# Denominators of a linear-attention pair: summed over partitions by a turn through memory instead of by TensorE

## The chip, the cores and the metric

One core of one Trainium2 chip runs the whole program. The metric is the device time of one execution in microseconds (us); the time given for a kernel is the median of several executions. Engines: TensorE (PE in the profile, PEld its weight loads), VectorE (DVE), ScalarE (ACT), GpSimd (POOL) and SyncE (SP). SP, ScalarE and GpSimd each have a queue from which they start transfers (DMA); all transfers share 16 DMA engines.

## The reference

Two independent attention blocks A and B, with S = 2048 rows, D = 640 and 32 heads of 20, whose outputs stand side by side:

```python
qkv = (x @ wqkv).reshape(B, S, 3, H, Dh).transpose(2, 0, 3, 1, 4)
phi = lambda t: where(t > 0, t + 1, exp(t)) + 1e-6
pq, pk = phi(q), phi(k)
kv  = einsum("bhsd,bhse->bhde", pk, v);  z = einsum("bhsd->bhd", pk)
num = einsum("bhqd,bhde->bhqe", pq, kv)
den = einsum("bhqd,bhd->bhq", pq, z)[..., None] + 1e-6
out = (num / den).transpose(0, 2, 1, 3).reshape(B, S, D) @ wo
```

The denominator `den` is one number for each row and head: a sum over 20 products of phi(q) and z.

## The kernel before

Every large product is made of three TensorE products of numbers cut into a high and a low part (tiles ending in h and l). The first 285 us build keys, values and z for both blocks, and the matrix M = kv times wo. The part that matters here comes after: eight units u = 0 to 7 (`NU` = 8), each of 512 rows, four of block A and four of block B.

For each unit there are two stretches on TensorE.

- The q stretch (`qmm`, L912 to L914): five column blocks c, each with five steps k of three products into one bank `psq`. ScalarE and VectorE make phi of each block (`qphi`), and `qacc` adds phi times z over the blocks into `acc[u]`, 128 partitions x 512 rows. The weights are ordered so that a partition p holds head p modulo 32: the denominator of head h is the sum of partitions h, h+32, h+64 and h+96 of `acc`.
- The o stretch (`outmm`, L1191): the division result times M, in 14 steps s = 0 to 13 of 6 products (s 0 to 5) or 9 products (s 6 to 13). The products of half q of the rows accumulate in the bank pa[q]. After steps 0 and 1, 4 and 5, 8 and 9, 10 and 11 ScalarE copies that bank out (L1206, `o<-pa`), and the accumulation goes on in it: step 10 writes the bank that the copy after step 8 reads, and step 11 the one of the copy after step 9.

The program runs q(u), then o(u-1): so after q(1) comes o(0), after q(2) comes o(1). The denominator of unit v is made during o(v-1), the stretch behind its own q stretch, and is used in o(v), one stretch pair later. The order is written by hand: `at(("o", w, s), f, ...)` puts a step f behind step s of o(w), and `run` calls it there. Each engine works off its own instructions strictly in that order.

The steps for one unit before:

- `split_acc`: ScalarE rounds `acc` (L906 `ac<-acc`), VectorE takes the remainder (L903).
- `denmm`: two TensorE products with `same`, a 128 x 128 matrix that is 1 where two partitions have the same head (L1102, L1103). The bank `psd` then holds the denominator in all four partitions of the head, for all 512 rows.
- `recip`: two VectorE reciprocals of 256 columns (L1108) into `rd`.
- `divide`: two VectorE products of 5 x 256 columns (L1114) on phi(q).
- Then `d_sums`, `a_split`, `d_split` prepare the left factors of o(v).

`round_xq` (L950 `xqh<-xqs`) rounds the next unit's input on ScalarE after steps 4, 6, 8, 10 and 12; q of the next unit needs the five results one after the other from its start on. SP loads these inputs (`xqs`, L943) and their low parts (`xql`, L947).

Each transfer of SP and of ScalarE raises one of eight semaphores, DMAHW0 to DMAHW7, which are handed out in turn over both queues. A transfer that takes a semaphore first waits until the earlier transfer with the same one has landed.

Of the kernel before, what the change touches and what calls it, by code (L numbers as in the profile page):

```python
# [7 lines left out]
F32 = mybir.dt.float32  # L8
# [3 lines left out]
AF = mybir.ActivationFunctionType  # L12
OP = mybir.AluOpType

H = 32
# [60 lines left out]
class Plan:  # L76
# [9 lines left out]
    def note(self, engine, n, fn, w, r, ahead=None, dma=None, late=None, by=None, due=None, safe=0.0):  # L86
        base = self.RATE.get(engine)
        j = Job(engine, base[0] + base[1] * n if base else n, fn, ahead, dma)
        for part, writes in [(p, True) for p in w] + [(p, False) for p in r]:
            sp = part.space  # L90
            if sp.where is not None and sp not in j.spaces:
                j.spaces.append(sp)
            for lo, hi, other, wrote in sp.uses:
                if lo < part.hi and part.lo < hi and (writes or wrote) and other is not j:
                    j.deps.add(other)
            if writes:
                sp.uses = [u for u in sp.uses if not (part.lo <= u[0] and u[1] <= part.hi and u[2] is not j)]
# [12 lines left out]
        self.jobs.append(j)  # L110
        return j
# [104 lines left out]
def tile_linear_attn_pair(ctx: ExitStack, tc: tile.TileContext, ins, out: bass.AP):  # L216
    nc = tc.nc
    P = 128
# [7 lines left out]
    NU = NB * NG  # L226
# [7 lines left out]
    dram = ctx.enter_context(tc.tile_pool(name="dram", bufs=1, space=bass.MemoryType.DRAM))  # L234
# [3 lines left out]
    kx, kg, q1a, q1b, q2, q3 = [], [], [], [], [], []  # L238
# [430 lines left out]
    a, z, x = jh[0][0:P], jl[0][0:P], jr[0][0:P]  # L669
# [117 lines left out]
    for p in range(4, NPB):  # L787
        i, h = divmod(p - 2, 2)
# [9 lines left out]
    for p in range(NPB + 2, NP):  # L798
        i, h = divmod(p - NPB - 2, 2)
# [17 lines left out]
    j = note("HOST", 0.0, swap, [gate.all], [])  # L817
# [51 lines left out]
    for g, (h0, nh) in enumerate(GROUPS):  # L869
        cols = NC * DH * nh  # L870
        w = Space("wv", cols, (BD,))
# [17 lines left out]
    def bank(name, tag="one", bufs=3):  # L889
        at, n = ptags[tag]  # L890
        pn[tag] = pn.get(tag, -1) + 1
        return psum.tile([P, 512], F32, name=name, tag=f"bank{at + pn[tag] % n}", bufs=1)
# [163 lines left out]
            nc.sync.dma_start(f32(t)[:, cs], d)  # L1056

    pq, acc, den, dd = {}, {}, {}, {}

    def qmm(u, c):  # L1060
        b = u // NG
        ps = bank("psq")
        cs = slice(c * P, (c + 1) * P)
        for k in range(NC):
            wh, wl = whl["q", b, k]
            xh, xl = xt[u, k]
            mm3(ps, wh[:, cs], wl[:, cs], xh, xl, k == 0, k == NC - 1)
            run("q", u, c, k)
        if c == NC - 1:
            for k in range(NC):  # L1070
                xt.pop((u, k))
        return ps
# [26 lines left out]
    def denmm(u):  # L1099
        t = acc.pop(u)  # L1100
        ps = den.pop(u) if u in den else bank("psd", "small", 1)
        nc.tensor.matmul(ps, same, t[:, 0], start=True, stop=False)  # L1102
        nc.tensor.matmul(ps, same, t[:, 1], start=False, stop=True)  # L1103
        den[u] = (ps, q2[0].tile([P, 512], F32, name="rd", tag="rd", bufs=1))

    def recip(u, h):
        ps, r = den[u]
        nc.vector.reciprocal(r[:, h * 256:(h + 1) * 256], ps[:, h * 256:(h + 1) * 256])  # L1108
# [169 lines left out]
    h = NG - 1  # L1278
# [8 lines left out]
    for c in range(NC):  # L1287
# [3 lines left out]
        for u in range(1, NU - 1):  # L1291
# [5 lines left out]

    chain = {
        0: [(("q", 1, 0, 0), split_acc, 0), (("q", 1, 1, 1), denmm, 0), (("q", 1, 1, 1), recip, 0, 0),
            (("q", 1, 1, 1), recip, 0, 1), (("q", 1, 1, 2), divide, 0, 0), (("q", 1, 1, 4), divide, 0, 1),  # L1300
            (("q", 1, 2, 0), d_sums, 0, 0), (("q", 1, 2, 2), a_split, 0, 0), (("q", 1, 2, 4), d_sums, 0, 1),
            (("q", 1, 3, 1), d_split, 0, 0), (("q", 1, 3, 4), a_split, 0, 1), (("q", 1, 4, 1), d_split, 0, 1)]}
    for v in range(1, NU):
        w, u = v - 1, v + 1
        if v == NU - 1:
            chain[v] = [(("o", w, 1), split_acc, v), (("o", w, 4), denmm, v), (("o", w, 4), recip, v, 0),
                        (("o", w, 5), divide, v, 0), (("o", w, 6), a_split, v, 0, 0), (("o", w, 6), d_sums, v, 0, 0),
                        (("o", w, 7), d_split, v, 0, 0), (("o", w, 8), a_split, v, 1, 0), (("o", w, 8), d_sums, v, 1, 0),
                        (("o", w, 9), recip, v, 1), (("o", w, 10), d_split, v, 1, 0), (("o", w, 12), divide, v, 1),
                        (("o", v, 0), a_split, v, 0, 1), (("o", w, 13), d_sums, v, 0, 1),  # L1310
                        (("o", v, 0), d_split, v, 0, 1), (("o", v, 2), d_sums, v, 1, 1),
                        (("o", v, 2), a_split, v, 1, 1), (("o", v, 3), d_split, v, 1, 1)]
        elif v == 1:
            chain[v] = [(("o", w, 4), split_acc, v), (("o", w, 7), denmm, v), (("o", w, 8), recip, v, 0),
                        (("o", w, 10), recip, v, 1), (("o", w, 11), divide, v, 0),
                         (("o", w, 12), divide, v, 1), (("q", u, 0, 2), d_sums, v, 0), (("q", u, 0, 4), a_split, v, 0),
                         (("q", u, 1, 2), d_sums, v, 1), (("q", u, 2, 1), d_split, v, 0), (("q", u, 3, 1), a_split, v, 1),
                         (("q", u, 3, 4), d_split, v, 1)]
        else:
            chain[v] = [(("o", w, 2), split_acc, v), (("o", w, 5), denmm, v), (("o", w, 7), recip, v, 0),  # L1320
                        (("o", w, 9), recip, v, 1), (("o", w, 11), divide, v, 0),
                         (("o", w, 12), divide, v, 1), (("q", u, 0, 2), d_sums, v, 0), (("q", u, 0, 4), a_split, v, 0),
                         (("q", u, 1, 2), d_sums, v, 1), (("q", u, 2, 1), d_split, v, 0), (("q", u, 3, 1), a_split, v, 1),
                         (("q", u, 3, 4), d_split, v, 1)]
    for v in range(NU):
        for a, f, *x in chain[v]:
            at(a, f, *x)
# [63 lines left out]
```

## Time and profile before

| | |
|---|---|
| time, median of 3 runs (571.76 to 574.32) | 573.65 us |
| the profiled execution's own time | 574.53 us |
| its span, first to last instruction | 572.8 us |
| TensorE busy | 565.7 us, 99% |
| VectorE busy | 434.3 us, 76% |
| ScalarE busy | 341.4 us, 60% |
| GpSimd busy | 57.2 us, 10% |
| granted TensorE clock | 0.999 |

The 1.73 us between the profiled execution's time and its span lie before the first and behind the last instruction. A unit's q and o stretches together take 33.34 us in the middle of the second part.

### The profile page before, as it was taken

Reading aid. Unit: us, or ns where it says so; the run is one execution under the profiler, and the core shown is the slowest. Engines: PE = TensorE matmul, PEld = TensorE weight load, DVE = VectorE, ACT = ScalarE, POOL = GpSimd, SP = SyncE. Lnnn points to the kernel's source line nnn. Section 1 sums busy time; section 2 is a strip of 40 time slices with the busy share of each in tenths; the row PEclk is TensorE's granted clock in tenths of the full one; section 3 lists DMA queues with packets and bytes.
Section 4 is the critical chain, followed back from the end, with each engine's and each line's share of the span. In section 5 each row is a group of like instructions: output and inputs, shape, how many; then the busy total and the mean of one; then the engine's idle time right before and its main releaser. Section 6 shows DMA issues by size and latency. Waiting matters only on the chain.

```text
span 572.8 us, 9505 instructions
## 1 busy us (share of the span) xinstructions
PE 565.7 (99%) x3524; PEld 535.8 (94%) x3524; DVE 434.3 (76%) x706; ACT 341.4 (60%) x619; POOL 57.2 (10%) x93
## 2 busy tenths in 40 slices
PE   8999999999999999999999999999999999999997
PEld 6999999999999999999988899898989989898997
DVE  6788687599888589976555699967788786758792
ACT  6877566673786677655156665646556464644551
POOL 0210011110010011100000103120012201001010
PEclk9999999999999999999999999999999999999999
DMA  8994665758858889786787986663363996122022
GB/s 296 379 242 141 163 183 128 205 143 246 278 144 217 250 249 321 216 252 196 211 245 275 339 276 215 226 218 109 120 225 134 355 390 231 47 76 93 0 93 92
DMA packets 69441, 117.64 MB, mean 205 GB/s; under 512 B 7956, under 2 KB 31252, under 8 KB 69396
## 3 DMA queue, kind: packets, MB, share of 16 engines
q1 hardware_dynamic: 60500, 89.98, 48.2%
q0 software_dynamic: 8608, 26.88, 16.7%
q8 instruction: 27, 0.44, 0.3%
q10 hardware_dynamic: 288, 0.20, 0.1%
q14 instruction: 18, 0.15, 0.1%
HBM read 71.13 MB, written 35.41 MB: 186 GB/s over the span
## 4 chain that ended last, share of the span: by engine, by line
PE 89%; DMA 5%; DVE 3%; ACT 1%; issue 1%; SPq 1%; ACTq 0%; DVEq 0%
PE psg L312 20%; PE pa L1191 12%; PE ka L312 8%; PE psq L912 8%; PE psq L914 8%; PE psq L913 8%; PE pe L1191 6%; PE ke L312 4%; PE psk L711 4%; PE psb L1191 4%; PE kb L312 3%; DMA md<-mev 2%; DMA wk<-in_A_wk 1%; PE pskv L551 1%; PE pskv L972 1%; DMA xqs<-in_A_xt 1%
## 5 line engine op out<-in xcount | busy, mean ns | idle before, releaser
L312 PE MATMUL psg<-pkl,xnh 128*128 128x320 f32 x320 | 98.9, 309 | 0.0
L312 PE MATMUL psg<-pkh,xnh 128*128 128x320 f32 x320 | 98.8, 309 | 0.0
L312 PE MATMUL psg<-pkh,xnl 128*128 128x320 f32 x320 | 98.4, 308 | 0.0
L912 PE MATMUL psq<-xqh,wh 128*128 128x512 f32 x200 | 78.6, 393 | 1.0 <-ACT xqh L860 1.0
L914 PE MATMUL psq<-xqh,wl 128*128 128x512 f32 x200 | 78.0, 390 | 0.0
L913 PE MATMUL psq<-xql,wh 128*128 128x512 f32 x200 | 77.9, 390 | 0.0
L312 PEld LDWEIGHTS psg<-pkl,xnh 128*128 128x128 f32 x320 | 60.1, 188 | 0.0
L312 PEld LDWEIGHTS psg<-pkh,xnl 128*128 128x128 f32 x320 | 60.1, 188 | 0.0
L312 PEld LDWEIGHTS psg<-pkh,xnh 128*128 128x128 f32 x320 | 60.0, 188 | 0.0
L1206 ACT ACTIVATE o<-pa 128x320 f32<-128x320 f32 x64 | 27.9, 438 | 45.2 <-PE pa L1191 45.0
L484 ACT ACTIVATE kt<-ka 128x320 f32<-128x320 f32 x52 | 22.6, 435 | 52.2 <-PE ka L312 49.0
L1082 DVE SCALAR_TENSOR_TENSOR pq<-eq,rq 128x512 f32<-128x512 f32 x40 | 27.6, 691 | 30.7 <-ACT rq L1081 30.6
L401 POOL DMA_DIRECT2D zacc<-ek x32 | 26.4, 836 | 244.5 <-DVE ek L494 185.3
L532 DVE TENSOR_TENSOR gacc<-psg,gacc 128x320 f32<-128x320 f32 x60 | 29.4, 489 | 28.1 <-PE psg L312 27.3
L1080 ACT ACTIVATE eq<-psq 128x512 f32<-128x512 f32 x40 | 23.9, 597 | 36.6 <-PE psq L914 34.2
L912 PEld LDWEIGHTS psq<-xqh,wh 128*128 128x128 f32 x200 | 37.6, 188 | 8.5 <-ACT xqh L860 1.3
L914 PEld LDWEIGHTS psq<-xqh,wl 128*128 128x128 f32 x200 | 37.5, 188 | 7.9
L913 PEld LDWEIGHTS psq<-xql,wh 128*128 128x128 f32 x200 | 37.6, 188 | 7.2
L396 ACT ACTIVATE pkh<-ek,epst 128x640 fp32r<-128x640 f32 x32 | 26.5, 829 | 7.9 <-DVE ek L494 7.5
L1191 PE MATMUL pa<-fh,dah 128*128 128x320 f32 x96 | 29.7, 309 | 0.0
L1191 PE MATMUL pa<-fh,dal 128*128 128x320 f32 x96 | 29.7, 309 | 0.0
L1191 PE MATMUL pa<-fl,dah 128*128 128x320 f32 x96 | 29.7, 309 | 0.0
(213 smaller groups left out, 1553.3 us busy)
## 6 DMA issues: line engine op xcount, KB each, us to landing
zacc<-ek POOLq DMA_DIRECT2D x32, 320.0 KB, 5.8
xql<-xd SPq DMA_DIRECT2D x40, 256.0 KB, 5.9
xd<-xl SPq DMA_DIRECT2D x29, 320.0 KB, 6.2
out<-o POOLq DMA_DIRECT2D x28, 320.0 KB, 3.6
xns<-in_A_x SPq DMA_DIRECT2D x16, 320.0 KB, 5.8
xts<-in_B_xt_tiles SPq DMA_DIRECT2D x16, 320.0 KB, 4.3
xns<-in_B_x SPq DMA_DIRECT2D x16, 320.0 KB, 5.1
xqs<-in_A_xt SPq DMA_DIRECT2D x20, 256.0 KB, 6.0
```

Of the source, the lines that this page charges most:

```text
L312: nc.tensor.matmul(o, a.r, w.r, start=start and k == i == 0, stop=k == n - 1 and i == 2, skip_group_check=True)
L396: note("ACT", n + 110, lambda: act(hi.r, p.f, AF.Identity, bias=epst), [hi], [p, K0.all], by=8.0)
L401: note("POOL", 1.0, lambda: nc.gpsimd.dma_start(z.f, p.f, **kw), [z], [p], dma=1.0 if first else 1.86)
L532: tt(o, BK[k].tile[:, :HF], o, op=OP.add)
L711: nc.tensor.matmul(o[h][:, :HF], x[a].r, w[c][h * HF:h * HF + HF].r, start=c == 0 and i == 0, stop=c == NC - 1 and i == 2, skip_group_chec ...
L912: nc.tensor.matmul(o, whi, xhi, start=first, stop=False)
L913: nc.tensor.matmul(o, whi, xlo, start=False, stop=False)
L914: nc.tensor.matmul(o, wlo, xhi, start=False, stop=last)
L1080: nc.scalar.activation(e, ps, AF.Exp)
L1082: nc.vector.scalar_tensor_tensor(pq[u][:, c, :], e, 1.0, r, op0=OP.min, op1=OP.add)
L1191: nc.tensor.matmul(ps, x, y, start=start and n == i == 0, stop=n == len(terms) - 1 and i == 2, skip_group_check=True)
L1206: copy = lambda x, y: nc.scalar.activation(x, y, AF.Copy)
```

## The change

For units 1 to 6 the sum over the four partitions is made in another way. Units 0 and 7 keep `split_acc`, `denmm` and `recip`.

- `acc_out`: one transfer from ScalarE's queue writes `acc` (128 x 512, 256 KB) to a tensor `ad` in memory.
- `acc_turn`: four transfers from ScalarE's queue read it back, each into 32 partitions, 64 KB in runs of 512 bytes. Partition q*32+h then holds, for head h and for the 128 rows of quarter q, the four numbers that belong together, side by side.
- `acc_add`: VectorE adds 256 columns to 256 columns, then 128 to 128, and takes the reciprocal of 128 columns.
- `spread`: each quarter's 32 x 128 reciprocals are copied to the four groups of 32 partitions of `rd`. VectorE makes the eight copies of quarters 2 and 3, ScalarE the eight of quarters 0 and 1.
- `divide` stays, one step later for the second half.

```diff
+    def acc_out(u):
+        nc.scalar.dma_start(ad[u], acc[u])
+        den[u] = (None, q2[0].tile([P, 512], F32, name="rd", tag="rd", bufs=1))
+
+    def acc_turn(u):
+        v = ad[u].rearrange("(k h) (q j) -> q h k j", k=4, q=4)
+        for q in range(4):
+            nc.scalar.dma_start(acc[u][q * H:q * H + H].rearrange("p (k j) -> p k j", k=4), v[q])
+
+    def acc_add(u):
+        t = acc[u]
+        nc.vector.tensor_tensor(t[:, :256], t[:, :256], t[:, 256:], op=OP.add)
+        nc.vector.tensor_tensor(t[:, :P], t[:, :P], t[:, P:256], op=OP.add)
+        nc.vector.reciprocal(t[:, :P], t[:, :P])
+
+    def spread(u, g, copy):
+        t = acc[u][g * H:g * H + H, :P]
+        for k in range(4):
+            copy(den[u][1][k * H:k * H + H, g * P:g * P + P], t)
...
-        elif v == 1:
-            chain[v] = [(("o", w, 4), split_acc, v), (("o", w, 7), denmm, v), (("o", w, 8), recip, v, 0),
-                        (("o", w, 10), recip, v, 1), (("o", w, 11), divide, v, 0),
-                         (("o", w, 12), divide, v, 1), (("q", u, 0, 2), d_sums, v, 0), (("q", u, 0, 4), a_split, v, 0),
...
-            chain[v] = [(("o", w, 2), split_acc, v), (("o", w, 5), denmm, v), (("o", w, 7), recip, v, 0),
-                        (("o", w, 9), recip, v, 1), (("o", w, 11), divide, v, 0),
...
+            o = 1 if v == 1 else 0
+            chain[v] = [(("o", w, 3 + o), acc_out, v), (("o", w, 6 + o), acc_turn, v), (("o", w, 10), acc_add, v),
+                        (("o", w, 10), spread_v, v, 2), (("o", w, 11), spread_v, v, 3),
+                        (("o", w, 11), spread_a, v, 0), (("o", w, 11), spread_a, v, 1),
+                        (("o", w, 12), divide, v, 0), (("o", w, 13), divide, v, 1),
```

What stands on the engines is shown at three places. In the rows, `psb` and `pa` are banks of the o stretch, and a name in brackets is a semaphore that the instruction waits for (DMAHW: transfers of SP and ScalarE; DMASW: of GpSimd).

TensorE in o(0), between steps 7 and 8, before:

```order
L1191 MATMUL psb<-fh,dah 128x320
L1191 MATMUL psb<-fl,dah 128x320
L1191 MATMUL psb<-fh,dal 128x320
L1102 MATMUL psd<-ac,same 128x512
L1103 MATMUL psd<-ac,same 128x512
L1191 MATMUL pa<-fh,dsh 128x320
L1191 MATMUL pa<-fl,dsh 128x320
```

and now (the line of `outmm` has become L1222):

```order
L1222 MATMUL psb<-fh,dah 128x320
L1222 MATMUL psb<-fl,dah 128x320
L1222 MATMUL psb<-fh,dal 128x320
L1222 MATMUL pa<-fh,dsh 128x320
L1222 MATMUL pa<-fl,dsh 128x320
```

The two products with `same` are gone, and nothing takes their place; the same holds in o(1) to o(5).

ScalarE in o(0), from the copy after step 4 to the rounding after step 8, before:

```order
L1206 ACTIVATE o<-pa 128x320 [waits PE_49]
L950 ACTIVATE xqh<-xqs 128x512 [waits DMAHW7_49]
L906 ACTIVATE ac<-acc 128x512 [waits DVE_49]
L1206 ACTIVATE o<-pa 128x320 [waits PE_49]
L950 ACTIVATE xqh<-xqs 128x512 [waits DMAHW0_49]
L906 ACTIVATE fsh<-wst 128x640 [waits DMAHW1_49,DVE_49]
L1206 ACTIVATE o<-pa 128x320 [waits DMASW4_49,PE_49]
L950 ACTIVATE xqh<-xqs 128x512
```

and now:

```order
L1237 ACTIVATE o<-pa 128x320 [waits PE_49]
L950 ACTIVATE xqh<-xqs 128x512 [waits DMAHW7_49]
L1108 DMA ad_3790<-acc 128x512 [waits DMAHW7_49,DVE_49]
L1237 ACTIVATE o<-pa 128x320 [waits PE_49]
L950 ACTIVATE xqh<-xqs 128x512 [waits DMAHW0_49]
L906 ACTIVATE fsh<-wst 128x640 [waits DMAHW1_49,DVE_49]
L1115 DMA acc<-ad_3790 32x4x128 [waits DMAHW7_49,DMAHW0_49]
L1115 DMA acc<-ad_3790 32x4x128
L1115 DMA acc<-ad_3790 32x4x128 [waits DMAHW2_49]
L1115 DMA acc<-ad_3790 32x4x128 [waits DMAHW3_49]
L1237 ACTIVATE o<-pa 128x320 [waits DMASW4_49,PE_49]
L950 ACTIVATE xqh<-xqs 128x512
```

The store stands where the rounding of `acc` stood; the four turned loads stand ahead of the copy after step 8, and the first of them waits until the store has landed (DMAHW7).

ScalarE in o(3), from the rounding of a form of M to the copy after step 8, now:

```order
L906 ACTIVATE fsh<-wst 128x640 [waits DMAHW1_49,DMASW6_49]
L1108 DMA ad_3793<-acc 128x512 [waits DMAHW6_49,DVE_49]
L1237 ACTIVATE o<-pa 128x320 [waits PE_49]
L950 ACTIVATE xqh<-xqs 128x512 [waits DMAHW2_49]
L1237 ACTIVATE o<-pa 128x320 [waits PE_49]
L950 ACTIVATE xqh<-xqs 128x512 [waits DMAHW3_49]
L1115 DMA acc<-ad_3793 32x4x128 [waits DMAHW6_49]
L1115 DMA acc<-ad_3793 32x4x128 [waits DMAHW4_49]
L1115 DMA acc<-ad_3793 32x4x128
L1115 DMA acc<-ad_3793 32x4x128 [waits DMAHW0_49]
L1237 ACTIVATE o<-pa 128x320 [waits DMASW4_49,PE_49]
```

where before stood:

```order
L906 ACTIVATE ac<-acc 128x512 [waits DVE_49]
L906 ACTIVATE fsh<-wst 128x640 [waits DMAHW2_49,DMASW6_49]
L1206 ACTIVATE o<-pa 128x320 [waits PE_49]
L950 ACTIVATE xqh<-xqs 128x512 [waits DMAHW3_49]
L1206 ACTIVATE o<-pa 128x320 [waits PE_49]
L950 ACTIVATE xqh<-xqs 128x512 [waits DMAHW4_49]
L1206 ACTIVATE o<-pa 128x320 [waits DMASW4_49,PE_49]
```

The fourth turned load of unit 4 takes DMAHW0, which the first of the five `xql` loads for unit 5 had before it: ScalarE cannot go on before that load of SP has landed. The rounding of the form (`fsh`) has moved ahead of the step that waits for `acc`.

More of the change, by code (lines that the diff above doesn't have):

```diff
@@ L1058, in tile_linear_attn_pair @@
     pq, acc, den, dd = {}, {}, {}, {}
+    ad = {u: dram.tile([P, 512], F32, name=f"ad{u}") for u in range(1, NU - 1)}
     def qmm(u, c):
@@ L1104, in denmm, with spread_a, spread_v @@
         den[u] = (ps, q2[0].tile([P, 512], F32, name="rd", tag="rd", bufs=1))
+    def acc_out(u):
[14 more added lines that the diff above has]
+            copy(den[u][1][k * H:k * H + H, g * P:g * P + P], t)
+        if g == 1:
+            acc.pop(u)
+    def spread_a(u, g):
+        spread(u, g, lambda y, x: nc.scalar.activation(y, x, AF.Copy))
+    def spread_v(u, g):
+        spread(u, g, nc.vector.tensor_copy)
     def recip(u, h):
@@ L1312, in tile_linear_attn_pair @@
                         (("o", v, 2), a_split, v, 1, 1), (("o", v, 3), d_split, v, 1, 1)]
-        elif v == 1:
-            chain[v] = [(("o", w, 4), split_acc, v), (("o", w, 7), denmm, v), (("o", w, 8), recip, v, 0),
-                        (("o", w, 10), recip, v, 1), (("o", w, 11), divide, v, 0),
-                         (("o", w, 12), divide, v, 1), (("q", u, 0, 2), d_sums, v, 0), (("q", u, 0, 4), a_split, v, 0),
-                         (("q", u, 1, 2), d_sums, v, 1), (("q", u, 2, 1), d_split, v, 0), (("q", u, 3, 1), a_split, v, 1),
-                         (("q", u, 3, 4), d_split, v, 1)]
-        else:
-            chain[v] = [(("o", w, 2), split_acc, v), (("o", w, 5), denmm, v), (("o", w, 7), recip, v, 0),
-                        (("o", w, 9), recip, v, 1), (("o", w, 11), divide, v, 0),
-                         (("o", w, 12), divide, v, 1), (("q", u, 0, 2), d_sums, v, 0), (("q", u, 0, 4), a_split, v, 0),
-                         (("q", u, 1, 2), d_sums, v, 1), (("q", u, 2, 1), d_split, v, 0), (("q", u, 3, 1), a_split, v, 1),
-                         (("q", u, 3, 4), d_split, v, 1)]
+        else:
+            o = 1 if v == 1 else 0
[3 more added lines that the diff above has]
+                        (("o", w, 12), divide, v, 0), (("o", w, 13), divide, v, 1),
+                        (("q", u, 0, 2), d_sums, v, 0), (("q", u, 0, 4), a_split, v, 0),
+                        (("q", u, 1, 2), d_sums, v, 1), (("q", u, 2, 1), d_split, v, 0), (("q", u, 3, 1), a_split, v, 1),
+                        (("q", u, 3, 4), d_split, v, 1)]
     for v in range(NU):
```

## The prediction

> **What bounds the kernel now.** The page comes first, for the engine that is full. Then TensorE's list of waits, then busy times by stretch, for whether it is full where the change is made.
>
> ```profile
> span 572.8 us, 9505 instructions
> PE 565.7 (99%) x3524; PEld 535.8 (94%) x3524; DVE 434.3 (76%) x706; ACT 341.4 (60%) x619; POOL 57.2 (10%) x93
> ...
> PE psq L912 <- ACT xqh L860: 1.0, 1, 1.0
> ...
> 370.33:386.64 16.31, 16.31 (x112) 16.22 (x111) 11.71 (x16) 7.99 (x17) 3.20 (x6) 1.00 0.69 235
> 386.64:403.67 17.03, 17.03 (x77) 14.08 (x77) 12.77 (x18) 9.16 (x14) 0.58 (x2) 1.00 0.27 91
> ```
>
> TensorE is busy 565.7 of 572.8 us, and the longest wait in its list is one of 1.0 us, on a tile of the program's opening of the second part (L860). The last two rows are o(1) and q(3): 16.31 of 16.31 us and 17.03 of 17.03, at a granted clock of 1.00 (the columns are length, then PE, PEld, DVE, ACT, POOL, clock, DMA share, GB/s). So here each TensorE instruction removed is time won, and each wait put in front of TensorE is time lost. The other engines have room: over these 33.34 us ScalarE works 17.15 and VectorE 24.48.
>
> **What goes.** TensorE loses two products for each of six units. What they cost is read between starts, since products overlap:
>
> ```profile
> 375.31 0.30 PE L1191 MATMUL pa<-fh,dsl 128*128 128x320 f32 x1
> 375.45 0.40 PE L1102 MATMUL psd<-ac,same 128*128 128x512 f32 x1
> 375.69 0.39 PE L1103 MATMUL psd<-ac,same 128*128 128x512 f32 x1
> 375.92 0.31 PE L1191 MATMUL psb<-fh,dah 128*128 128x320 f32 x1
> ```
>
> From 375.45 to 375.92 is 0.47 us for the pair, so 6 x 0.47 = 2.8 us. This is all that the change can win, since nothing else on TensorE gets shorter. It is 0.49% of 573.65 us; below 0.5%, about 2.9 us, a measurement of this kernel can hardly be told from no change.
>
> **VectorE and ScalarE.** The grouped lines give the removed work and the nearest to the added work:
>
> ```profile
> L1108 DVE RECIPROCAL rd<-psd 128x256 f32<-128x256 f32 x16 | 27.8, 1746 | 0.9 <-PE psd L1103 0.9
> L903 DVE TENSOR_TENSOR ac<-acc,ac 128x512 fp32r<-128x512 f32 x8 | 5.5, 692 | 4.9 <-ACT ac L906 4.9
> L906 ACT ACTIVATE ac<-acc 128x512 fp32r<-128x512 f32 x8 | 5.0, 631 | 5.3 <-DVE acc L1092 5.3
> L903 DVE TENSOR_TENSOR dal<-pq,dah 128x128 fp32r<-128x128 f32 x2 | 0.6, 284 | 0.0
> L906 ACT ACTIVATE dah<-pq 128x128 fp32r<-128x128 f32 x2 | 0.6, 300 | 0.0
> ```
>
> VectorE loses 2 x 1.75 + 0.69 = 4.2 us a unit. It gets a sum of 256 columns (between 0.28 and 0.69, say 0.45), one of 128 (0.28), a reciprocal of 128 columns (half of 1.75, 0.87): 1.6 us for `acc_add`; and eight copies of 128 columns at no more than 0.28, at most 2.3 us. That is 3.9 against 4.2: no loss. ScalarE loses 0.63 and gets eight copies at 0.30 (2.4, less where they overlap) and five transfer issues; with 0.44 for each issue (below) that is 4.6, so 4.0 more a unit, against 16.2 us of idle time in 33.34. As work, all this is hidden under TensorE. The second half's division moves some 2 us back; what it feeds is read by TensorE only in the next o stretch, a whole q stretch (17.03 us) later. Only order and waiting can cost.
>
> **The new wait on ScalarE.** The first turned load waits for the store to land, and it stands ahead of ScalarE's copy after step 8. Step 10 writes the bank that this copy empties. So the copy must be done when step 10 begins, two steps after the start of step 8, that is 2.64 us behind the starts below, less the 0.47 that go. The chain of waits gives the start of step 8 for units 1 to 6 (the first number), and ScalarE's timeline the moment at which `acc` is ready: the start of the rounding `ac`, which becomes the store. In unit 3 (the third of them) a rounding of weights now stands ahead, and the store starts at about 407.05. The last three rows are ScalarE's copy, its rounding of weights and its `round_xq`.
>
> ```profile
> 345.38 5.28 PE pa L1191 x36
> 378.71 5.28 PE pa L1191 x36
> 412.06 5.28 PE pa L1191 x36
> 445.39 5.28 PE pa L1191 x36
> 478.74 5.28 PE pa L1191 x36
> 512.08 5.28 PE pa L1191 x36
> ...
> 343.23 0.63 ACT L906 ACTIVATE ac<-acc 128x512 fp32r<-128x512 f32 x1 [0.85 <-DVE acc L1092]
> 373.25 0.63 ACT L906 ACTIVATE ac<-acc 128x512 fp32r<-128x512 f32 x1 [0.68 <-DVE acc L1092]
> 406.44 0.62 ACT L906 ACTIVATE ac<-acc 128x512 fp32r<-128x512 f32 x1
> 440.17 0.64 ACT L906 ACTIVATE ac<-acc 128x512 fp32r<-128x512 f32 x1 [0.92 <-DVE acc L1092]
> 473.02 0.63 ACT L906 ACTIVATE ac<-acc 128x512 fp32r<-128x512 f32 x1 [0.43 <-DVE acc L1092]
> 506.36 0.63 ACT L906 ACTIVATE ac<-acc 128x512 fp32r<-128x512 f32 x1 [0.43 <-DVE acc L1092]
> ...
> L1206 ACT ACTIVATE o<-pa 128x320 f32<-128x320 f32 x64 | 27.9, 438 | 45.2 <-PE pa L1191 45.0
> L906 ACT ACTIVATE wh<-wst 128x640 fp32r<-128x640 f32 x5 | 3.7, 731 | 0.2 <-DMA wst<-in_B_wq 0.2
> L950 ACT ACTIVATE xqh<-xqs 128x512 fp32r<-128x512 f32 x35 | 21.6, 624 | 0.0
> ```
>
> Unit 1: step 10 begins at 345.38 + 2.64 - 0.47 = 347.55. The copy takes 0.44 and TensorE's release about 0.1 by my estimate, so it must start by 347.0; four issues of 0.45 ahead of it take 1.8, so the store must have landed by 345.2. It starts at 343.23: it has 2.0 us. In the same way unit 2 has 4.85 (a rounding as wide as the copy, 0.44, stands between), unit 3 4.1 (one of 0.73), unit 4 5.0, units 5 and 6 5.5. Unit 1 is so short because VectorE is late with `acc` there, and because its steps stand one place later.
>
> How long landing takes, by the nearest rows:
>
> ```profile
> L650 ACTq DMA_DIRECT2D xj<-in_A_xt x2: 402/438/474, 0.7 to 1.2; - x2
> out<-o POOLq DMA_DIRECT2D x28, 320.0 KB, 3.6
> xql<-xd SPq DMA_DIRECT2D x40, 256.0 KB, 5.9
> out<-o SPq DMA_DIRECT2D x3, 320.0 KB, 2.1
> 343.20:345.70 2.50, 2.50 (x18) 2.41 (x17) 1.77 (x4) 1.63 (x4) 0.00 (x0) 1.00 0.00 0
> 473.00:477.00 4.00, 4.00 (x28) 3.91 (x28) 0.69 (x1) 2.46 (x5) 0.00 (x0) 1.00 0.97 358
> ```
>
> An issue on ScalarE's queue takes 0.44. Stores to memory land after 2.1 us at the end, where nothing else moves, and 3.6 in the median; loads of the store's own size among others take 5.9. Unit 1's store meets a DMA share of 0.00, so I take 2.4, near the lowest row: a stall of 0.4. Bounds are 0.1 (2.1 us) and 3.9 (5.9 us). For the other units I take the stores' 3.6, which is inside all margins: 0.
>
> [...]
>
> **The new wait on SP's load.** In unit 4 the fourth turned load waits until the first `xql` load for unit 5 has landed.
>
> ```profile
> 442.76 0.38 SPq L947 DMA_DIRECT2D xql<-xd  x1
> ...
> DMA to landing us min/median/max: 6.3/6.3/6.3
> ...
> 441.47 0.82 DVE L903 TENSOR_TENSOR fsl<-wst,fsh 128x640 fp32r<-128x640 f32 x1
> ```
>
> The load was issued at 442.76, and the one landing that is recorded among the five took 6.3 us: until 449.06. SP waits there for VectorE's `fsl`, which can now start at about 440.15, since both roundings of `acc` ahead of it are gone: 1.3 us earlier. So the load lands at about 447.75. The fourth issue should begin by 447.0 - 0.45 = 446.57 (step 10 at 447.56, copy by 447.02). That is a stall of 1.2 us. Bounds: 0, if this load lands in 5 us, and 2.5, if nothing starts earlier. The queued copy after step 8 is the one that TensorE waits for; the roundings and copies behind it have a step of room each.
>
> **The turned loads.** VectorE must not wait so long in `acc_add` that ScalarE's `spread`, and behind it the last `round_xq`, come late for q: that result is read 12 products, 2.7 us, into the q stretch. The nearest row has the same 32-partition form, though far fewer bytes:
>
> ```profile
> L603 SPq DMA_DIRECT2D zq<-zd x8: 383/432/477, 197.2 to 290.9; - x8
> ...
> DMA to landing us min/median/max: 2.9/3.6/4.4
> ```
>
> q(3) starts at 386.64, so 389.36 less 0.47, less 0.55 for the rounding (0.62 with its overlap), 1.7 for eight copies that overlap, 1.6 for `acc_add` and 0.6 of releases: the loads must land by 384.4, 5.7 us behind the start of step 8. In unit 2 the fourth issue ends at about 378.7, which leaves 5.7; unit 1 and unit 4, whose issues end at 347.4 and 448.2, have 4.1 each with their stalls counted. 3.6 and 4.4 us straddle that; I take 3.6 and 0, bounds 0 and 2.2 (6.3 us) in unit 4.
>
> **The sum.** -2.8 + 0.4 + 1.2 = -1.2 us. The profiled execution took 574.53 (572.8 span and 1.73 around it), so 573.3 of its kind. It lay 0.9 above the median of 573.65; against that median, 572.5.
>
> **Rivals.** *Everything is covered*: the `xql` load lands in 5 us and the store in 2.1. Time 573.65 - 2.8 = 570.9. For it speaks that ScalarE has half its time free; against it, unit 1's 2.0 us.
>
> *Stores land late, and the kernel gets slower.* ScalarE stands before the first turned load in every unit, and TensorE before step 10. At 5.0 us the stalls are 3.0, 0.15 and 0.9 in units 1 to 3 with 1.2 in unit 4: 5.25, a time of 576.1. At 6.2 they are 4.2, 1.35, 2.1, 1.2, 0.7 and 0.7: 10.25, a time of 581.1. It eats the gain from 3.6 us on (1.6 in unit 1 and 1.2 in unit 4) and makes the kernel slower by over 2.9 from 5.2. For it: 5.9 for `xql`, a share of 0.97 in unit 5. Against it: unit 1, where it costs most, has no other traffic.
>
> *Turned loads land late.* Beyond 4.1 us each further us in units 1 and 4 is one us of TensorE waiting at the start of q for `xqh`. At 6.3 us in both that is 4.4: 572.5 + 4.4 = 576.9. For it: unit 4's loads run beside the twenty loads of M's forms. Against it: even the slowest `zq` took 4.4. [...]
>
> **How the numbers follow.** Forecast, a part eaten: 0.50, with 571.2 to 574.5 of its own. Covered: 0.14, of which 0.12 falls beyond the bound because executions scatter (571.76 to 574.32 before). Late stores: 0.22, 0.18 of it over the bound. Late loads: 0.14, 0.10 over it. Faster 0.12; slower 0.28; the rest, 0.60, within. The range runs from 570.5, full cover with the scatter of runs, to 580, late stores at nearly 6 us; little lies outside.
>
> **What would show it.** Right: no `psd` products in o(0) to o(5); TensorE waits in step 10 on ScalarE's `o<-pa`, in o(0) and o(3) alone; stretches of 15.8 us elsewhere. Wrong: waits of TensorE on `xqh` at the start of q (late loads); step 10 waiting in o(1), o(2), o(4) too (late stores); ScalarE issues well over 0.44.

## The result, and the profile after

The changed kernel takes 580.07 us, median of 6 runs (578.75 to 582.2), against 573.53 us for the kernel before in 6 runs of the same session (571.76 to 574.8): ratio 1.0121, 95% interval 1.0093 to 1.0148. It is slower by some 6.5 us, where 1.2 us less were forecast. Its profiled execution took 579.72 us, 5.2 us more than that of the kernel before.

The head of the page:

```profile
span 577.9 us, 9628 instructions
PE 565.4 (98%) x3512; PEld 535.2 (93%) x3512; DVE 432.4 (75%) x754; ACT 350.9 (61%) x661; POOL 57.3 (10%) x93
```

and the first row of TensorE's list of waits (us in total, times, longest):

```profile
PE pa L1222 <- ACT o L1237: 4.9, 3, 3.7
```

This row is new: TensorE waits three times for ScalarE's copy of a bank. The 12 `psd` products are gone (3524 instructions to 3512), yet TensorE is busy almost as long as before, 565.4 us against 565.7. So some of its products have become slower.

Busy times by stretch show where. Three rows of the kernel before, o(0), o(2) and o(3):

```profile
336.70:353.13 16.43, 16.43 (x111) 16.22 (x110) 15.53 (x22) 10.80 (x22) 2.25 (x4) 1.00 0.59 197
...
403.55:419.85 16.30, 16.30 (x112) 16.21 (x111) 13.08 (x18) 10.75 (x21) 1.08 (x2) 1.00 0.63 203
...
436.85:453.15 16.30, 16.30 (x111) 16.20 (x110) 12.30 (x17) 8.62 (x18) 3.78 (x8) 1.00 0.70 240
```

and of the changed kernel o(0), o(1), o(2), the q stretch behind it, o(3) and o(4):

```profile
337.79:354.59 16.80, 16.24 (x109) 15.85 (x108) 14.18 (x30) 10.48 (x25) 2.25 (x4) 1.00 0.66 220
...
371.62:388.33 16.71, 16.11 (x109) 15.85 (x108) 9.42 (x22) 8.66 (x22) 2.70 (x5) 1.00 0.80 281
...
405.36:421.20 15.84, 15.84 (x110) 15.84 (x108) 9.86 (x18) 10.11 (x21) 1.08 (x2) 1.00 0.70 221
421.20:438.25 17.05, 17.05 (x77) 14.00 (x76) 15.85 (x27) 11.80 (x23) 2.16 (x4) 1.00 0.40 138
438.25:459.61 21.36, 17.65 (x110) 17.38 (x108) 11.89 (x23) 9.58 (x23) 4.31 (x8) 0.92 0.81 258
...
476.64:492.49 15.85, 15.85 (x110) 15.84 (x109) 7.72 (x19) 8.43 (x21) 1.08 (x2) 1.00 0.79 268
```

o(2), o(4) and o(5) are 0.46 us shorter than before, the gain that was forecast for the two products. o(0) is 0.4 longer than before; o(1), 16.30 before, is 0.4 longer too; o(3) is 5.06 longer, and its granted clock is 0.92. Over the six o stretches that is +0.37 +0.41 -0.46 +5.06 -0.45 -0.46 = +4.5 us. What is left of the 5.2 is 1.1 us ahead of o(0), which begins at 337.79 instead of 336.70, less 0.4 behind o(5). The start of o(0) scatters from run to run, between 334.5 and 338.0 in the kernels below, whose programs do not differ up to there.

In o(3) two things happen one behind the other. The chain of waits there:

```profile
445.21 6.55 DMA xql<-xd
...
451.78 0.31 ACTq L1115
```

ScalarE's timeline, where the four turned loads stand as one row:

```profile
447.71 4.39 ACTq L1115 DMA_DIRECT2D acc<-ad  x4
452.19 0.44 ACT L1237 ACTIVATE o<-pa 128x320 f32<-128x320 f32 x1 [5.89 <-DMA xql<-xd]
```

and TensorE's:

```profile
448.67 0.31 PE L1222 MATMUL pa<-fh,dal 128*128 128x320 f32 x1
452.69 0.47 PE L1222 MATMUL pa<-fh,dah 128*128 128x320 f32 x1 [3.71 <-ACT o L1237]
452.96 0.47 PE L1222 MATMUL pa<-fl,dah 128*128 128x320 f32 x1
```

The fourth turned load goes out at 451.78, when the first of SP's five `xql` loads has landed (445.21 + 6.55 = 451.76). Only then can ScalarE make the copy behind it, and TensorE, whose last product began at 448.67, goes on at 452.69: 3.9 us more than the usual 0.147 from start to start. From there the products start 0.267 us apart for some 13 products, and that is another 1.6 us.

### The profile page after: what moved, and what is told of

It reads as the page before. It is cut to its first block, busy times and chain, and to the rows that moved or that the text cites. A ratio compares the mean times of both kernels' runs of the same rounds, so it can differ in the third digit from the quotient of the medians.

```text
span 577.9 us, 9628 instructions
## 1 busy us (share of the span) xinstructions
PE 565.4 (98%) x3512; PEld 535.2 (93%) x3512; DVE 432.4 (75%) x754; ACT 350.9 (61%) x661; POOL 57.3 (10%) x93
## 4 chain that ended last, share of the span: by engine, by line
PE 70%; DVE 12%; DMA 9%; ACT 4%; issue 2%; ACTq 1%; SPq 1%; DVEq 0%
PE psg L312 20%; PE ka L312 8%; PE pa L1222 8%; PE psq L912 5%; PE psq L914 5%; PE psq L913 5%; PE ke L312 4%; PE psk L711 4%; PE pe L1222 4%; PE kb L312 3%; DMA md<-mev 3%; PE psb L1222 2%; DVE pq L1083 2%; DMA xqs<-in_B_xt 1%; DMA ad<-acc 1%
## 5 line engine op out<-in xcount | busy, mean ns | idle before, releaser
L1222 PE MATMUL pa<-fh,dah 128*128 128x320 f32 x96 | 30.7, 319 | 4.9 <-ACT o L1237 4.9
L1238 DVE TENSOR_TENSOR o<-pe,o 128x320 f32<-128x320 f32 x32 | 15.6, 489 | 22.0 <-ACT o L1237 19.2
L1222 PE MATMUL pa<-fl,dah 128*128 128x320 f32 x96 | 30.4, 317 | 0.0
```

Of the source, the lines that this page charges most:

```text
L1222: nc.tensor.matmul(ps, x, y, start=start and n == i == 0, stop=n == len(terms) - 1 and i == 2, skip_group_check=True)
```

## The experiments

Each time stands against the kernel before on the same chip in the same session (medians 573.4 to 574.1 us). "Turned" means that a unit uses the way through memory; the other units keep TensorE's two products.

**Unit 4 alone set back.** Units 1, 2, 3, 5, 6 turned:

```diff
-    ad = {u: ... for u in range(1, NU - 1)}
+    ad = {u: ... for u in (1,2,3,5,6)}
+        elif v not in (1,2,3,5,6):
+            chain[v] = [(("o", w, 2), split_acc, v), ...
```

> Unit 4 alone gets its denominator from TensorE again; units 1, 2, 3, 5 and 6 stay changed. Theory (ScalarE's fourth turned load of unit 4 waits for SP's first xql load, TensorE stands 3.9 us behind it and then runs 3.5 us at half clock): o(3) takes 16.3 us again instead of 21.36, clock 1.00; the other stretches as in the changed kernel, so -0.6 us against before, about 573. Rival A (the loss is spread out: the added transfers slow everything, the part ahead of o(0) too, which took 1.1 us longer in the changed kernel's profile): it stays above 577.

Measured: 577.62 us (574.31 to 581.43), ratio 1.0072 (1.0041 to 1.0103). So unit 4 accounts for only a part. In this profile, the slowest of its runs, TensorE waits 2.3 us in o(0), 1.7 in o(1) and 0.4 in o(4), because the store takes longer than in the changed kernel. ScalarE's timeline in o(0) and o(1):

```profile
343.39 0.34 ACTq L1108 DMA_DIRECT2D ad<-acc  x1
...
347.44 1.78 ACTq L1115 DMA_DIRECT2D acc<-ad  x4
...
376.96 0.34 ACTq L1108 DMA_DIRECT2D ad<-acc  x1
...
383.36 1.76 ACTq L1115 DMA_DIRECT2D acc<-ad  x4
```

From the store's issue to the first turned load it is 4.1 and 6.4 us. And o(3), with its old products, takes 18.2 us instead of the 16.3 expected, with two waits on `ac` (1.24 and 0.49 us): `acc` of unit 4 is late although unit 4 is as before.

**Unit 4 alone turned.** The same edit with `(4,)`.

> Only unit 4 is changed; the others are as before. Theory with its second half (the load that ScalarE waits for was late because VectorE was behind from unit 3, whose turned loads came late): acc is ready about 2.5 us earlier in o(3), the xql load is issued some 5 us after the start of o(3) instead of 7, and step 10 waits 0 to 1.5 us, clock 1.00: 573 to 575. Rival B (the wait is unit 4's own, whatever came before): step 10 waits 3 to 4 us again and the clock falls, o(3) takes 21 us: 578 to 579.

Measured: 576.33 us (575.02 to 577.6), ratio 1.0054 (1.0037 to 1.0070). TensorE's only wait for the copy is 2.4 us by its list, 2.56 over the usual distance of starts, and the half rate follows: o(3) takes 20.06 us. The time lies between the two theories.

These 2.6 us are not simply unit 4's own part of the 3.9. With fewer transfers ahead of it, unit 4 gets other semaphores: its fourth turned load follows the second of SP's `xql` loads here, not the first. By the trace it goes out at 447.37, when that second load has landed (447.35); the first had landed at 446.28, 1.1 us before. Behind the first load, as in the changed kernel, some 1.5 us of wait would be left, as an estimate from these times.

**Unit 3 set back**, units 1, 2, 4, 5, 6 turned.

> Unit 3 keeps TensorE's sums, units 1, 2, 4, 5 and 6 are turned. Theory: of the 3.9 us of wait in unit 4's stretch some 1.3 are inherited from unit 3, whose fourth turned load waits for SP's `xqs` load and makes VectorE late; here the wait of o(3) is 2.4 to 2.8 as with unit 4 alone, o(2) is 16.3 again, so 579 (577.5 to 580) with 1.3 less in o(3) and 0.5 more in o(2). Rival: unit 4's wait is all its own (the load of `xql` comes at a fixed time and a turned load waits for it): o(3) stays at 21.4, 580.5.

Measured: 579.92 us (576.64 to 583.93), ratio 1.0105 (1.0068 to 1.0142). Both expected times lie inside that scatter, and the profile, of the fastest of its runs, has to answer: o(3) waits 2.58 us instead of 3.9, and o(2) is 16.3 again. So at least 1.3 us of unit 4's wait come from unit 3. VectorE's timeline shows how: its rounding `fsl`, which SP's loads wait for. In the kernel before, with unit 3 set back, and in the changed kernel (o(3) starts at 436.85, 436.08 and 438.25):

```profile
441.47 0.82 DVE L903 TENSOR_TENSOR fsl<-wst,fsh 128x640 fp32r<-128x640 f32 x1
```

```profile
439.29 0.82 DVE L903 TENSOR_TENSOR fsl<-wst,fsh 128x640 fp32r<-128x640 f32 x1
```

```profile
444.00 0.82 DVE L903 TENSOR_TENSOR fsl<-wst,fsh 128x640 fp32r<-128x640 f32 x1
```

It begins 4.6, 3.2 and 5.75 us into o(3). With unit 3 set back it is 1.4 us earlier than before, as the prediction had it (1.3); with unit 3 turned it is 1.1 later.

Unit 3's part is in fact larger than 1.3, because here too the fourth turned load follows the second `xql` load. SP's timeline has the issue of the first, and the chain of waits the second:

```profile
440.50 0.62 SPq L947 DMA_DIRECT2D xql<-xd  x1
```

```profile
441.16 7.15 DMA xql<-xd
```

The second landed at 448.31, and the turned load went out at 448.33. The first, by the trace, landed at 447.32. That is 11.2 us into o(3); in the changed kernel the same load landed 13.5 us into it (451.76). So unit 3 delays this load by 2.3 us, and the change of semaphore, 1.0 us, hides the difference between 2.3 and 1.3.

**Only units 5 and 6 turned.**

> Only units 5 and 6 are changed, whose o stretches took 15.85 us in the changed kernel and had no wait. Theory: -0.9 us against before, about 572.6. Rival A: if the mere presence of the change costs 1 to 2 us in the untouched part, 573.7 to 575.

Measured: 573.52 us (572.64 to 575.5, 12 runs), ratio 0.9999 (0.9984 to 1.0013). The two stretches:

```profile
471.11:488.02 16.91, 16.12 (x109) 15.85 (x108) 7.79 (x19) 8.30 (x21) 1.08 (x2) 1.00 0.80 276
505.06:520.91 15.85, 15.85 (x110) 15.85 (x109) 7.76 (x19) 8.44 (x21) 1.08 (x2) 1.00 0.31 107
```

Unit 6 wins 0.45 us at a DMA share of 0.31. Unit 5, at 0.80, waits here and loses 0.6, though it won 0.45 in the changed kernel at 0.79. The chain of waits in o(4) shows why:

```profile
469.89 4.96 DMA xqs<-in_B_xt
...
474.92 5.30 DMA ad<-acc
```

`acc` is ready at 473.91, but the store has the semaphore of one of SP's `xqs` loads and stands until that has landed (474.85). It goes out 3.8 us into o(4), in the changed kernel 2.8. The landing of 5.3 us alone would have fitted the margin of 5.5 us that the prediction gave unit 5; with the 1.0 us of the semaphore it does not. No other cost of the transfers shows: the two units cancel, and the time is that of the kernel before.

**All transfers from GpSimd's queue** (`nc.scalar.dma_start` becomes `nc.gpsimd.dma_start` in `acc_out` and `acc_turn`).

> The same change for units 1 to 6, but all five transfers are issued by GpSimd, whose transfers have semaphores of their own. ScalarE no longer waits for any transfer ahead of the copy after step 8. Theory: no wait of TensorE in o(0) to o(5), each 15.84 us, clock 1.00: -2.8 us against before, about 570.8. Rival A: 575 or more, since the transfers are still there. Rival C (the turned loads are late whoever issues them): TensorE waits for xqh at the start of a q stretch.

Measured: 581.76 us (580.45 to 583.88), ratio 1.0153 (1.0126 to 1.018). No o stretch waits any more (15.84 to 15.96 us), and the wait has moved to the start of q. TensorE's list:

```profile
PE psq L912 <- ACT xqh L950: 7.7, 3, 4.4
```

and the chain in front of q(5):

```profile
451.65 6.74 DMA acc<-ad
...
458.51 0.44 DVE acc L1119
...
462.52 0.31 ACT rd L1132
...
462.85 0.64 ACT xqh L950
...
463.53 0.79 PE psq L912
```

The turned loads land late, VectorE's sums come late, ScalarE's eight copies wait for them, and behind the copies in ScalarE's order stands the `xqh` that q needs. This is the forecast's rival "turned loads land late", brought out by another queue.

**GpSimd's queue and the tail behind step 13**, so that the last `xqh` is made first:

```diff
-(("o", w, 10), acc_add, v), ... (("o", w, 12), divide, v, 0), (("o", w, 13), divide, v, 1),
+(("o", w, 13), acc_add, v), (("o", w, 13), spread_v, v, 2), (("o", w, 13), spread_v, v, 3),
+(("o", w, 13), spread_a, v, 0), (("o", w, 13), spread_a, v, 1),
+(("q", u, 0, 0), divide, v, 0), (("q", u, 0, 1), divide, v, 1),
```

> All five transfers from GpSimd's queue, and VectorE's sums and reciprocal, both engines' copies and the two divisions set behind step 13, so that ScalarE makes its last `xqh` before it waits for anything turned. Theory: the transfers cost only through what stands behind them on ScalarE, the copies after steps 8 and 9 in the changed kernel and the last `xqh` in the GpSimd one. Then both kinds of wait of TensorE go, every o stretch is 15.8 to 16.0 us, and 570.7 (569.8 to 572) comes out, 2.8 under the kernel before. Rival: the late sums push VectorE over its 17.05 us per q stretch wherever they are put, the divisions arrive late for the next o stretch or the `phi` of a q stretch is late; then TensorE waits 1 to 4 us on VectorE in units 2 to 5 and 574 to 578 comes out.

Measured: 582.55 us (580.4 to 584.81), ratio 1.0145 (1.0118 to 1.0171). The rival comes nearest, at a higher price than its 574 to 578: TensorE waits on ScalarE, and ScalarE on VectorE's division. The waits on `xqh` are gone, and new ones stand at step 4 (0.87 and 2.43 us) and in the q stretch behind o(1). VectorE's timeline there:

```profile
390.00 0.42 DVE L1119 TENSOR_TENSOR acc<-acc 128x256 f32<-128x256 f32 x1 [2.71 <-DMA acc<-ad]
...
394.36 2.89 DVE L1145 SCALAR_TENSOR_TENSOR pq<-pq,rd 128x1280 f32<-128x1280 f32 x2 [0.74 <-ACT rd L1132]
```

ScalarE's:

```profile
397.29 1.06 ACT L906 ACTIVATE dah<-pq 128x1024 fp32r<-128x1024 f32 x1 [2.96 <-DVE pq L1145]
398.25 0.58 ACT L1081 ACTIVATE eq<-psq 128x512 f32<-128x512 f32 x1
```

The division ends at 397.25, the split `dah` waits for it, and ScalarE's first Exp of the q stretch stands behind the split. TensorE has both `psq` banks full by then, waits 2.5 us and goes on at 399.37.

**ScalarE's queue, turned loads behind the copies after steps 8 and 9** (`acc_turn` at `("o", w, 9)`), the same late tail.

> The transfers stay on ScalarE's queue, but the turned loads are issued behind the copies after steps 8 and 9 instead of ahead of them, with the same late tail. Theory: order alone cures it, 570.7 to 573 and no wait `PE pa <- ACT o`. Rival: ScalarE waits for the store of a unit with a late `acc` there too and the next thing in its order is late, the last `xqh` or the first Exp of the q stretch: then `PE psq <- ACT` waits of 2 to 4 us in units 1 and 4 and 575 to 579.

Measured: 585.38 us (584.22 to 586.05), ratio 1.0199 (1.0173 to 1.0226). The wait at step 10 is gone; `PE psq <- ACT rq` is 6.2 us in three waits, again the Exp behind the split, and the time lies above both theories' ranges. This other order does not cure it.

**The whole tail in the following q stretch**, from GpSimd's queue, turned loads into `rd`:

```diff
+(("q", u, 1, 0), acc_add, v), ... spread ..., (("q", u, 1, 2), divide, v, 0), (("q", u, 1, 4), divide, v, 1),
+(("q", u, 2, 0), d_sums, v, 0), (("q", u, 2, 2), a_split, v, 0), (("q", u, 2, 4), d_sums, v, 1),
+(("q", u, 3, 1), d_split, v, 0), (("q", u, 3, 4), a_split, v, 1), (("q", u, 4, 1), d_split, v, 1)
```

> All transfers from GpSimd's queue, the turned loads land in the tile `rd` (the sums then go into a 128x128 tile), and everything behind the landing is set where unit 0 has it, in the following q stretch behind its first `phi`: sums, reciprocal and copies before matmul group 1, divisions in group 1, differences and splits in groups 2 to 4. Theory: from `acc` to the first split the way through memory takes some 19 us (store 5, turned loads 4.5, sums and reciprocal 1.7, copies 2.5, divisions 2.9, differences 1.4, issue between them), more than an o stretch of 15.9; where it must end within one, some engine waits in its order, whichever queue is used. Given the q stretch too, nothing waits: all o stretches 15.9, all q stretches 17.05, 570.7 (569.8 to 572). Rival: VectorE has no room in the q stretch (15.1 of 17.05 us busy before); it arrives late for the next o stretch, TensorE waits 1 to 3 us in each of units 2 to 6 and 576 to 585 comes out.

and the same with the last split behind step 3 of the next o stretch (`a_split` at `("q", u, 4, 1)`, `d_split` at `("o", v, 3)`):

> As the one with the tail in the q stretch, and the last split of each unit (`dsh`, `dsl` of the second differences, read from step 8 on) put behind step 3 of the o stretch, where VectorE has 4 us to spare. Theory: same as that one, 570.7 (569.8 to 572.5). Rival of a full VectorE: this takes some 1.2 us per unit out of the q stretch and so 0.5 to 1 us off the waits of each of units 2 to 6: 2 to 5 us less than the other kernel; but `acc` comes later by the 1.2 us.

Measured: 593.48 us (592.11 to 596.03), ratio 1.0351 (1.0316 to 1.0385), and 590.18 us (589.28 to 591.29), ratio 1.0285 (1.0257 to 1.0312). My theory's time was wrong by some 20 us in both. TensorE's list of the first:

```profile
PE pe L1224 <- DVE dsl L903: 7.3, 6, 1.7
...
PE pa L1224 <- DVE dal L903: 1.9, 2, 1.7
```

VectorE's timeline of the second, in the q stretch behind o(1) and the start of o(2):

```profile
392.43 0.69 DVE L1083 SCALAR_TENSOR_TENSOR pq<-eq,rq 128x512 f32<-128x512 f32 x1 [4.05 <-ACT rq L1082]
...
406.65 1.22 DVE L903 TENSOR_TENSOR dsl<-sr,dsh 128x1024 fp32r<-128x1024 f32 x1
```

TensorE waits for VectorE's splits in six o stretches. VectorE stands idle for 4.05 us at the start of the q stretch, since its first `phi` is not there yet, works with hardly a pause from then on (14.4 of 15.4 us), and ends the split `dsl` at 407.9, when TensorE is already waiting for it. So the rival holds in its mechanism, though the time of the first lies above its 576 to 585: a late tail does not fit into the q stretch. The second kernel takes 3.3 us less, within the 2 to 5 expected, but its waits on `dsl` and `dal` are the same 7.3 and 1.9 us, because the split that was moved stands behind them in VectorE's order; the 3.3 us came from smaller waits.

**Store on ScalarE's queue, loads on GpSimd's, the split behind the first Exp** (the late tail with `d_sums`, `a_split` at `("q", u, 1, 0)` and `("q", u, 1, 1)`), once for units 1 to 6 and once for 2, 3, 5, 6:

> Store on ScalarE's queue, turned loads on GpSimd's, the late tail behind step 13, and the first differences and split of a unit moved from q group 0 to group 1, behind ScalarE's first Exp, so that this Exp no longer stands behind a split that waits for the divisions. Theory: the way through memory ends some 19 us after `acc`; the wait `PE psq <- ACT rq` of the late-tail kernels (2.4 to 3.3 us and half rate behind it) came from the order of that split and the Exp. Without it 571 to 574. Rival: VectorE's time is the bound, since it stands idle while the turned values are on their way and has to make all that follows in a q stretch that is already full; then the next thing in its order is late, TensorE waits on `dsl` or `dal` at the next o stretch, 576 to 586.

> The same with units 1 and 4 left to TensorE's sums, the two whose `acc` is ready last, and whose o stretches carry the loads of the next unit's `xql`. Theory: units with an early `acc` (2, 3, 5, 6) can take the way through memory, -0.47 each: 571.6 (570.5 to 573). Rival as for the other kernel: 574 to 580, with waits of TensorE on VectorE's `dsl` or on ScalarE in units 2, 3, 5 and 6.

Measured: 579.29 us (577.72 to 581.13), ratio 1.0106 (1.008 to 1.0132), and 577.79 us (574.98 to 578.66), ratio 1.0072 (1.0047 to 1.0096). The wait of the split and the Exp is gone, and the next thing is late. At step 4 of o(1), o(2), o(3) and o(5) TensorE waits 0.4 to 3.5 us for the copy after step 0, which stands behind ScalarE's last Exp, which waits for VectorE's `phi`. ScalarE's timeline of the first kernel at o(3), ahead of the longest of these waits:

```profile
440.30 0.60 ACT L1081 ACTIVATE eq<-psq 128x512 f32<-128x512 f32 x1 [0.89 <-DVE pq L1083]
...
441.27 0.78 ACT L1237 ACTIVATE o<-pa 128x320 f32<-128x320 f32 x2
```

With units 1 and 4 as before, o(3) still waits 2.2 us there. That unit 3 makes VectorE late for it is likely, but not shown by a run of its own. My theory is refuted in both. The rival's times hold, though not the waits on `dsl` and `dal` that it named. No version of these beats the kernel before.

**A wait without transfers.** The kernel before, with ScalarE's second `xqh` made 9 to 12 times over in four o stretches.

> The kernel before, with ScalarE's second `xqh` of the o stretches o(1), o(2), o(4) and o(5) made 10, 9, 11 and 12 times over, so that TensorE waits at step 10 for ScalarE's copy some 1.7, 2.1, 1.9 and 2.5 us with no transfer in it. Theory: TensorE's half rate after a wait depends on the length of the wait alone, from somewhere between 1.65 and 2.26 us on: the matmuls after the longest wait run at 0.267 us for about 3.5 us, those after the shortest at 0.147. Rival: it comes from the transfers or the unit's place: then no stretch shows 0.267. Time 573.5 + 8.2 + 1.6 for each wait that halves the rate: 583 to 588.

Measured: 594.65 us in one run. The waits are 2.78, 3.00, 3.08 and 3.74 us over the usual distance, longer than I had set them, and the half rate follows three of the four. Waits and half rate make some 18 of the 21 us; another 1.3 lie ahead of o(0), which begins at 337.98 instead of 336.70, and the rest is open. TensorE's timeline after the shortest and after the next:

```profile
385.26 0.41 PE L1194 MATMUL pa<-fh,dah 128*128 128x320 f32 x1 [2.62 <-ACT o L1209]
385.52 0.31 PE L1194 MATMUL pa<-fl,dah 128*128 128x320 f32 x1
...
421.71 0.58 PE L1194 MATMUL pa<-fh,dah 128*128 128x320 f32 x1 [2.84 <-ACT o L1209]
422.09 0.47 PE L1194 MATMUL pa<-fl,dah 128*128 128x320 f32 x1
```

So the half rate comes behind waits with no transfer in them too (3.00, 3.08 and 3.74 us), and the expectation that the length alone decides is too simple: 2.78 us did not bring it, shorter waits in other kernels did (2.16 to 2.69 us, last section).

## Why the prediction was wrong

**The gain was right.** 0.46 us in each o stretch without a wait, against 0.47 worked out. The instruction prices held too: VectorE is busy 432.4 us against 434.3 ("no loss"), a turned issue takes 0.443 in the median against 0.44 taken, and TensorE went on 0.05 us after ScalarE's copy in o(3), where 0.1 was taken.

**Unit 1 was nearly right.** The store landed after 2.35 us where 2.4 was taken, and TensorE waited 0.7 where 0.4 was forecast. The chain of waits:

```profile
344.31 2.35 DMA ad<-acc
...
374.94 5.28 DMA ad<-acc
```

The second row is unit 2, where 3.6 us was taken and 0 forecast: it landed after 5.28, over the margin of 4.85, and TensorE waited 0.8. So 3.6 us, from stores that GpSimd starts, was too short a price for units 2 and 5. The rival on late stores is a part of the loss, not the bulk.

**The step that failed is unit 4's term: 1.2 us forecast, bounds 0 to 2.5, and 3.9 + 1.6 = 5.5 measured.** The mechanism was the one named, the fourth turned load behind SP's first `xql` load. What the prediction had wrong is when that load lands: 10.9 us into o(3) by its sum, 13.5 us measured (451.76). It put the delay that unit 3 hands on through VectorE at nothing.

The start of `fsl` "1.3 us earlier" counted only the roundings that leave VectorE's order. Of the second half's division the prediction said that it "moves some 2 us back", and that this is hidden. In fact both halves of unit 3's division moved 3.4 us back, here the first of them before and after (14.4 and 17.8 us into o(2)):

```profile
417.98 1.48 DVE L1114 SCALAR_TENSOR_TENSOR pq<-pq,rd 128x1280 f32<-128x1280 f32 x1
```

```profile
423.17 1.49 DVE L1145 SCALAR_TENSOR_TENSOR pq<-pq,rd 128x1280 f32<-128x1280 f32 x1 [0.22 <-ACT rd L1132]
```

What the division feeds is indeed read only an o stretch later. But VectorE works in order, and behind the division stands all its work of the q stretch, at whose end come unit 4's `acc` and the `fsl` that SP waits for. The prediction read VectorE's room from o(1) and q(3), 24.48 of 33.34 us. The q stretch that the delay goes through, q(4), is fuller, in the kernel before:

```profile
419.85:436.85 17.00, 17.00 (x76) 14.05 (x76) 15.12 (x24) 10.41 (x16) 2.70 (x5) 1.00 0.42 154
```

In the changed kernel it had 17.05 - 15.85 = 1.2 us of room, so the delay was carried on: `fsl` came 2.5 us later than assumed, and the `xql` load landed 2.6 us later. With the 1.2 already forecast, these 2.6 us make the wait of 3.9. The prediction had looked only for the reader of the late result, not for what is queued behind it.

The kernel with unit 3 set back shows how much of this is unit 3's. There `fsl` begins 3.2 us into o(3), as assumed (3.3), and the first `xql` load lands 11.2 us into it. So 2.3 of the 2.6 us come from unit 3. The other 0.3 lie in the load itself: it took 6.8 us there (440.50 to 447.32), where the prediction relied on the one landing of 6.3. Unit 4's own part of the wait, some 1.5 us by the estimate from the kernel with unit 4 alone, is close to the 1.2 forecast.

Part of unit 3's delay is a wait for a semaphore that the prediction did not list. Its fourth turned load shares one with SP's load `xqs`:

```profile
410.01 4.14 DMA xqs<-in_B_xt
...
414.16 4.03 DMA acc<-ad
```

It went out at 414.16 and landed at 418.19, and VectorE's sums began at 418.8. No TensorE wait shows in unit 3, so it looks free; its price is paid in unit 4.

**The half rate was not foreseen.** It cost 1.6 us in o(3); the kernel before, with a mean clock of 0.999, gave no sign of it. Two columns of o(3)'s row above show it: a granted clock of 0.92, and 17.65 us of PE busy with two products less.

**What is shown and what is not.** Shown by experiment, with one profile each: that with unit 3 set back the load that held unit 4 lands 2.3 us earlier in o(3), that in the kernels tried the queue decides where the wait stands and not whether there is one, and that VectorE has no room for a later tail. That the shared semaphore holds the fourth load is read from the traces: in the changed kernel, with unit 4 alone and with unit 3 set back it goes out 0.02 us after the landing of that `xql` load which had its semaphore, the first once and the second twice. In the kernel before, the 322 transfers of SP and ScalarE bear eight semaphore numbers in the same turn throughout; in the changed kernel none of the 344 that take a number again went out before the earlier one had landed. Not tried was a kernel with these semaphores apart on ScalarE's queue, nor one with unit 3 set back and unit 4's semaphores as they were, so the 1.5 us or so that unit 4 would cost by itself stay an estimate.

Why the store of unit 1 took 2.35 us in the changed kernel and 4.0 with unit 4 set back can be read from the two traces. In the second a packet of 16 KB on the queue `instruction` runs from 344.43 to 345.93, in the middle of the store. Fifteen of the store's sixteen parts have landed by 345.37; packets of the last follow from 345.93 on, and it lands at 347.36. In the changed kernel such a packet begins at 346.12, when the store's data has been moved.

## What to carry to other kernels

When a short step of a full engine is replaced by a way through memory, count the whole way, from the last operand to the first reader, and ask of each engine on it what is queued behind its wait; an engine busy 75% overall can have little to spare where the delay arrives (VectorE 1.2 us in q(4)). A delay that shows no wait where it arises is passed on in order, so follow it into the next stage before pricing it at nothing. Taking transfers out dealt the shared semaphores out anew here (unit 4's fourth turned load followed SP's second `xql` load instead of the first): a kernel with one unit set back is not the changed kernel less that unit, until it is looked up which load each transfer now waits for. Moving the wait to another queue or slot changed the name in the list of waits (`o`, `xqh`, `rq`, `dsl`), not the sign of the result.

## What the runs showed of the hardware

After some waits TensorE's products run at half rate (0.267 us from start to start instead of 0.147 with 320 columns, 0.427 instead of 0.227 with 512). The traces' records of the granted clock have 0.50 there: for 3.4 us in twelve cases (in the changed kernel from 452.90 to 456.31) and for 6.8 us, twice that, in four, counted in all kernels above without the ends of the programs. This sets in at the earliest 1.6 us before the wait ends and at the latest 1.2 us behind it, one case with several waits aside. Single waits of 0.7 to 1.9 us over the usual distance were never followed by it. Between 2.1 and 2.8 both occur: 2.16, 2.26, 2.43, 2.54, 2.56, 2.58 and 2.69 us were followed by it, 2.17, 2.43 (step 4 of the late tail) and 2.78 (the copies) were not. From 3.0 us on (3.00 to 4.55) all eight were. So in these kernels the length alone does not decide below 3 us. Shorter waits close together brought it once: 1.2, 0.5 and 1.5 us within 6 us, in o(6) of the second kernel with the tail in the q stretch.

How long a store of 256 KB from ScalarE's queue takes goes with the traffic at that moment. In the changed kernel it landed after 2.35 us in unit 1, with a DMA share of 0.32 while it ran (its own packets included), after 5.28 us in unit 2 (1.02) and 5.03 in unit 5 (0.89). For the other units the first turned load, which waits for the landing, gives a bound: 2.7 us in units 3 and 6 (0.39 and 0.28), 3.6 in unit 4 (0.88). The same step can thus cost twice as much a few stretches later in the same program, and in unit 2 the difference was more than the whole margin.
